# Order of the first loads and of the first group's attention rounds in a one-core kernel: linear attention, then a gated feed-forward

## The chip, the cores and the metric

The kernel runs on one core of one Trainium2 chip. Its engines are PE (matrix products; PEld is the load of its weights), DVE (vector), ACT (activations), POOL, and SP, which here only issues DMAs. DMAs are issued from SP, ACT and POOL. The metric is the device time of one launch in microseconds (us), given as the median of several runs.

## The reference

```python
# q, k, v: 8 x 8 x 576 x 64 (batch, head, row, dim), float32
kv  = einsum('bhsd,bhse->bhde', k, v)          # 64 x 64 per head
out = einsum('bhsd,bhde->bhse', q, kv)
rms = sqrt(mean(out * out, axis=-1) + 1e-06)
x   = out / rms * g_norm                       # then to 4608 x 512
h   = x @ w_in                                 # 512 -> 2048, weights in float64
sp  = maximum(h, 0) + log1p(exp(-abs(h)))
y   = (h * erf(sp)) @ w_out                    # 2048 -> 512
```

## The kernel before, in words

The 4608 rows are worked in groups T. Groups 0 to 7 are the first 512 rows of the eight batches, group 8 gathers the last 64 rows of every batch. Two heads form a pair p, so each group has four pairs. For each group the kernel runs attention, then the two feed-forward products in pieces of 128 of the 2048 columns.

The weights come as float64. For the first group they are turned into float32 piece by piece beside the work: `load_w` fetches a raw piece (L192 for w_in, L197 for w_out), `w_split` takes exponent and mantissa apart (DVE L207, L216; ACT L215, L219), and `w_join` puts them together (DVE L226, L230, L240). Four raw buffers turn, so a load waits for the join four pieces earlier.

Attention of one pair consists of pieces, which the kernel issues one by one:

- `products` (L288): kv of the two heads, 12 products of 64x64 in one PSUM tile `kv_ps` (L297, in the trace 24 passes); for even pairs the transposition of the last 64 rows of two pairs, the tail (L305); DVE copies the two blocks into the block-diagonal `bd_kv` (L312) and the tail into `qT_last` (L315); PE transposes q (L319, four times), ACT copies it out (L320).
- `apply` (L322): the block-diagonal product with the tail (L324) and with q (L325, into `se_ps`); DVE copies the tail's result (L326), ACT squares (L328).
- `mean` (L341): a product with `mean_w` gives the mean of squares (L351); ACT does Ln, Exp and Square (L358, L359, L360).
- `norm` (L364): three DVE operations (L366, L369, L378); the last one writes `xT`.

There is no scheduler: each engine takes its instructions in the order in which the code issues them (`manual_schedule`). For group 0 that order is made by a loop over rounds i (L568):

```python
for i in range(NP + 3):
    for piece, p in ((0, i), (1, i - 1), (4, i - 3), (3, i - 2)):
```

So in round i come `products` of pair i, `apply` of pair i-1, `norm` of pair i-3 and `mean` of pair i-2 (piece 2 isn't used in group 0). After them come the weight steps of `w_rounds` (L559): the first split in round 1, the first join in round 2. The PSUM tiles of q's transposes and of the means share two banks in turn (`banks_0`); `se_ps` has a bank for each pair.

The first loads are issued as follows. `load_pair` (L120) issues q of a pair from SP (L127), and k and v (L136) from ACT for pairs 0 to 2 and from SP after that. `load_last` (L145) issues two heads' tails from SP (L147). POOL first fetches g_norm (L154), then makes the identity `ident` for the transposes, zeroes `bd_kv` (L180) and computes `gm_col` (L182). SP's order is q of pair 0, two tails, q of pairs 1 and 2, two raw pieces of w_in, two more tails, then q, k and v of pair 3. The built program gives the loads of SP and ACT eight completion semaphores in turn, so a load waits until the one eight before it has landed.

A load of q holds 256 KB, of k or v 288 KB, of a tail 32 KB, of a raw piece of w_in 512 KB (the first four) or 1024 KB.

Of the kernel before, what the change touches and what calls it, by code (L numbers as in the profile page):

```python
# [39 lines left out]
FP32 = mybir.dt.float32  # L40
# [20 lines left out]
def kernel(  # L61
# [10 lines left out]
    nc = tc.nc  # L72
    P = 128
    B, H, S, D = q.shape
    DM, DF = moe_w_in.shape[0], moe_w_in.shape[1] // 2
    J = 4
    G = J * P
    R = S - G
    NP = H // 2
# [5 lines left out]
    const = ctx.enter_context(tc.tile_pool(name="const", bufs=1))  # L85
# [12 lines left out]
    ps_o = ctx.enter_context(tc.tile_pool(name="ps_o", bufs=1, space=PSUM))  # L98
# [12 lines left out]
    q_sb, k_sb, v_sb = {}, {}, {}  # L111
# [4 lines left out]
    def chunks(T):  # L116

        return 6 if T == 0 else 5

    def load_pair(i):  # L120
        T, p = divmod(i, NP)
        if T >= B:
            return
        pool = early if i in (2, 3) else kvp
        side = nc.scalar if i < 3 else nc.sync
        t = q_sb[T, p] = pool.tile([P, J, 2, D], FP32, name="q_sb", tag="q")
        nc.sync.dma_start(  # L127
            out=t, in_=q[T, 2 * p : 2 * p + 2, 0:G, :].rearrange("h (p j) d -> p j h d", j=J)
        )
        for name, got, src in (("k", k_sb, k), ("v", v_sb, v)):  # L130
            C = chunks(T)
            rows, rest = divmod(S, C)
            assert rest < 2
            t = got[T, p] = pool.tile([rows + rest, 2, C, D], FP32, name=f"{name}_sb", tag=name)
            heads = src[T, 2 * p : 2 * p + 2]
            side.dma_start(  # L136
                out=t[:rows].rearrange("r h c d -> r h (c d)"),
                in_=heads[:, : S - rest].rearrange("h (r c) d -> r h (c d)", c=C),
            )
            if rest:  # L140
                side.dma_start(
                    out=t[rows:, :, 0], in_=heads[:, S - rest :].rearrange("h r d -> r h d")
                )

    def load_last(T, p):  # L145
        if T < B:
            nc.sync.dma_start(  # L147
                out=q_last[p % 2 * R : p % 2 * R + R, p // 2],
                in_=q[T, 2 * p : 2 * p + 2, G:S, :].rearrange("h r d -> r h d"),
            )  # L150

    g_col = const.tile([P, 1], FP32, name="g_col")
    for i in range(2):
        nc.gpsimd.dma_start(  # L154
            out=g_col[i * D : i * D + D, :], in_=g_norm.rearrange("(d one) -> d one", one=1)
        )
    for i in range(NP - 1):
        load_pair(i)
        if i == 0:
            load_last(0, 0)  # L160
            load_last(0, 1)

    w_in_sb = first_w.tile([P, KC, DF], FP32, name="w_in_sb")
    w_out_sb = first_w.tile([P, FC, DM], FP32, name="w_out_sb")
# [1 line left out]

    ident = const.tile([P, P], FP32, name="ident")
    make_identity(nc, ident)
    mean_w = const.tile([P, P], FP32R, name="mean_w")
    mean_f = early.tile([P, P], FP32, name="mean_f", bufs=1)  # L170
    nc.vector.memset(mean_f, 0.0)
# [4 lines left out]
    nc.vector.memset(exp_col, -896.0 * (1 << 23))  # L176
    eps_col = const.tile([P, 1], FP32, name="eps_col")
    nc.vector.memset(eps_col, EPS)
    bd_kv = const.tile([P, 2, P], FP32, name="bd_kv")
    nc.gpsimd.memset(bd_kv, 0.0)  # L180
    gm_col = const.tile([P, 1], FP32, name="gm_col")
    nc.gpsimd.tensor_scalar(out=gm_col, in0=g_col, scalar1=-0.5, scalar2=None, op0=ALU.mult)  # L182
    x_last = const.tile([P, KC, G], FP32, name="x_last")
# [66 lines left out]
    def w_next(what):  # L250
        i = w_at[what]
        if i < len(w_order):
            w_at[what] = i + 1
            {"load": load_w, "split": w_split, "join": w_join}[what](*w_order[i][1:])
# [14 lines left out]
    def attention(T, p, pools=None):  # L269

        st = {}

        halves = FIRST <= T < B
        bd = bd_kv[:, (T * NP + p) % 2, :]

        q_tail, o_tail = slice(P, 2 * P), slice(2 * P, 2 * P + R)

        def bank(name):
            pool, tag = (pools or {}).get(name, (ps_at, "at"))
            return pool.tile([P, G], FP32, name=name, tag=tag)  # L280

        def square_tile(name):

            if T == 0:
                return gate.tile([P, G], FP32, name=name, tag="h")
            return attp.tile([P, G], FP32, name=name, tag="qT")

        def products():  # L288

            kv_ps = st["kv"] = bank("kv_ps")  # L290
            ks, vs, qs = (x.pop((T, p)) for x in (k_sb, v_sb, q_sb))
            C = chunks(T)
            for c in range(C):
                rows = slice(0, S // C + (c < S % C))
                for i in range(2):
                    s = slice(i * D, i * D + D)
                    nc.tensor.matmul(  # L297
                        kv_ps[s, s],
                        lhsT=ks[rows, i, c],
                        rhs=vs[rows, i, c],  # L300
                        start=(c == 0),
                        stop=(c == C - 1),
                    )
            if p % 2 == 0:
                nc.tensor.transpose(kv_ps[:, q_tail], q_last[:, p // 2], ident)  # L305
            if p == NP - 2:
                for i in range(NP):
                    load_last(T + 1, i)
            st["qT"] = square_tile("qT")
            for i in range(2):  # L310
                s = slice(i * D, i * D + D)
                nc.vector.tensor_copy(out=bd[s, s], in_=kv_ps[s, s])  # L312
            if p % 2 == 0:
                tails[T] = attp.tile([P, P], FP32, name="qT_last", tag="t")
                nc.vector.tensor_copy(out=tails[T], in_=kv_ps[:, q_tail])  # L315
            st["tail"] = tails[T][:, p % 2 * R : p % 2 * R + R]
            qt_ps = bank("qt_ps")
            for j in range(J):
                nc.tensor.transpose(qt_ps[:, j * P : j * P + P], qs[:, j], ident)  # L319
            nc.scalar.copy(st["qT"], qt_ps)  # L320

        def apply():  # L322
            qT, o_ps, kv_ps = st["qT"], bank("se_ps"), st.pop("kv")
            nc.tensor.matmul(kv_ps[:, o_tail], lhsT=bd, rhs=st.pop("tail"), start=True, stop=True)  # L324
            nc.tensor.matmul(o_ps, lhsT=bd, rhs=qT, start=True, stop=True)  # L325
            nc.vector.tensor_copy(out=x_last[:, p, T * R : T * R + R], in_=kv_ps[:, o_tail])  # L326
            st["o"] = o_ps
            nc.scalar.activation(qT, o_ps, AF.Square)  # L328
# [62 lines left out]
        def loads():  # L391
            load_pair(T * NP + p + 2)

        if T == 0:
            return products, apply, halve, mean, norm
        if T == B:
            return lambda: None, square, lambda: None, mean, norm, split

        pieces = ((products,), (apply,), (halve, loads)) if halves else ((products, loads), (apply,), ())
        return (*(partial(chain, *group) for group in pieces), mean, norm, split)  # L400

# [112 lines left out]
    o_ps = {}  # L514
# [34 lines left out]
    def unit(name):  # L549
        return gate.tile([P, G], FP32, name=name, tag=name[0])  # L550


    for _ in range(2):
        w_next("load")
    load_last(0, 2)
    load_last(0, 3)
    load_pair(NP - 1)

    w_rounds = {  # L559
        1: ("split",),  # L560
        2: ("join", "load", "split"),
        3: ("join", "load"),
        5: ("split",),
        6: ("split", "join", "load", "join", "load"),
    }
    banks_0 = {"kv_ps": (ps_at, "at"), "qt_ps": (ps_h, "h"), "ms_ps": (ps_h, "h")}
    first = [attention(0, p, banks_0 | {"se_ps": (ps_o, f"o{p}")}) for p in range(NP)]
    for i in range(NP + 3):  # L568
        for piece, p in ((0, i), (1, i - 1), (4, i - 3), (3, i - 2)):
            if 0 <= p < NP:  # L570
                first[p][piece]()
        if i == 1:
            for _ in range(RAW - 2):
                w_next("load")
            load_pair(NP)
            load_pair(NP + 1)
        for what in w_rounds.get(i, ()):
            w_next(what)
# [65 lines left out]
    for n in range(FIRST * FC + 1):  # L644
        T, f = divmod(n, FC)
# [33 lines left out]
        elif T < FIRST:  # L679
# [10 lines left out]
            for i, c in blocks:  # L690
                nc.tensor.matmul(  # L691
                    plain[i],
                    lhsT=w_in_sb[:, c, i % FC * P : i % FC * P + P],
                    rhs=xT[T][:, c, :],
                    start=(c == 0),
                    stop=(c == KC - 1),
                )
        if T < FIRST:
            if n == whole:
                old_h = acc.tile([P, BATCH, G], FP32, name="h", tag="e")  # L700
            h = hs[n] = old_h[:, n - whole] if n >= whole else unit("h_sb")
# [51 lines left out]
    def part(h, half):  # L753
        return h[:, :, half * 2 * P : half * 2 * P + 2 * P]
# [31 lines left out]
    for m in range(first_batch, batches + 1):  # L786
        T, b = divmod(m, NB)
        todo = []
        if T + 1 < NG:
            todo = list(attention(T + 1, b))  # L790
            if b == 0:
                side = late_r if T % 2 == FIRST % 2 else late
# [28 lines left out]
        if m < batches:  # L821

            pool, tag = (acc, "e") if m % 2 else (wide, "b")
            h = pool.tile([P, BATCH, G], FP32, name="h", tag=tag)
# [22 lines left out]
        for j in range(J):  # L847
# [7 lines left out]
            for half in range(2) if j == 1 and m < batches - 1 else (j,) if j < 2 and m == batches - 1 else ():  # L855
                nc.vector.tensor_tensor(  # L856
                    out=part(h, half), in0=part(h, half), in1=part(s, half), op=ALU.mult
# [38 lines left out]
```

## Time and profile before

| | |
|---|---|
| Runs | 946.79, 948.34, 949.3, 949.31 us |
| Median | 948.82 us |
| Profiled execution | 946.79 us, its span 945.0 us |
| PE, DVE, ACT, POOL busy | 926.1, 740.1, 615.5, 2.4 us |
| Granted PE clock, mean | 0.999 |
| DMA in the span | 259.78 MB, mean 275 GB/s |
| PE busy in 0 to 20, 20 to 40, 40 to 60 us | 11.24, 17.96, 20.00 us |

The times of the profile are from the start of the span of 945.0 us; the run around it took 1.8 us more. PE is the busiest engine, 98% of the span, and most of what it lacks is lost at the start. A busy share is an average over the whole span, so stages have to be looked at one by one. A timeline line gives start, duration, engine, code line, operation, what is written and read, the count of merged instructions, and in brackets the idle time before it and what ended it. A line of windows gives for each engine the busy time in a stretch and the number of instructions, then the granted clock, the mean busy share of the 16 DMA engines and the rate in GB/s.

### The profile page before, as it was taken

What the parts mean: (1) busy time and instruction counts of PE and PEld (TensorE: products, weight loads), DVE (VectorE), ACT (ScalarE), POOL (GpSimd) and SP (SyncE); (2) the same over time, 40 slices, a digit from 0 to 9 for tenths busy, and PEclk for the clock granted to TensorE, in tenths of its full rate; (3) what the DMA queues carried; (4) which work ended last, traced back from release to release, by engine and by line L of the source; (5) the groups of instructions that cost most, each with busy time, mean ns of one, the idle gap of its engine ahead of it and who ended that gap; (6) DMA issues with size and microseconds to landing.
All of it is one profiled execution on the core that took longest, in us unless ns stands there. A gap on an engine that the chain in (4) does not pass through costs nothing.

```text
span 945.0 us, 11743 instructions
## 1 busy us (share of the span) xinstructions
PE 926.1 (98%) x4272; PEld 683.1 (72%) x4272; DVE 740.1 (78%) x1054; ACT 615.5 (65%) x825; POOL 2.4 (0%) x10
## 2 busy tenths in 40 slices
PE   6999999999999999999999999999999999999998
PEld 4444445665688888888888888888888888878886
DVE  3979958888577788777788888878887877777667
ACT  4889876777666666666666666666666666665552
POOL 1000000000000000000000000000000000000000
PEclk9999999999999999999999999999999999999999
DMA  9856505899699998998899889988797779768872
GB/s 261 283 166 214 162 7 219 309 343 339 221 339 339 310 332 293 315 313 278 291 295 316 290 295 313 313 302 293 266 339 272 265 250 348 286 246 310 335 271 60
DMA packets 111842, 259.78 MB, mean 275 GB/s; under 512 B 43864, under 2 KB 69544, under 8 KB 111784
## 3 DMA queue, kind: packets, MB, share of 16 engines
q1 hardware_dynamic: 110152, 256.73, 78.5%
q10 hardware_dynamic: 1568, 2.29, 0.8%
q8 instruction: 34, 0.56, 0.2%
q14 instruction: 24, 0.20, 0.1%
q0 software_dynamic: 64, 0.00, 0.0%
HBM read 224.40 MB, written 34.60 MB: 274 GB/s over the span
## 4 chain that ended last, share of the span: by engine, by line
PE 87%; ACT 5%; DVE 5%; DMA 2%; issue 1%; SPq 0%; DVEq 0%
PE n_ps L462 45%; PE m_ps L462 23%; PE o_ps L520 8%; PE h_ps L691 3%; PE se_ps L325 3%; PE kv_ps L297 2%; PE qt_ps L319 1%; DMA w_raw<-in_moe_w_in_dram 1%; ACT w_e L215 1%; ACT w_m L219 1%; DMA v_sb<-in_v_dram 1%; PE ms_ps L346 1%; PE ms_ps L347 1%; ACT L103 1%; ACT s_sb L719 1%
## 5 line engine op out<-in xcount | busy, mean ns | idle before, releaser
L462 PE MATMUL n_ps<-x_forms,w_in_parts 128*128 128x512 f32 x896 | 233.2, 402 | 1.5 <-DVE x_forms L408 0.7
L462 PE MATMUL n_ps<-w_out_parts,g_forms 128*128 128x512 f32 x928 | 231.3, 391 | 0.0
L462 PEld LDWEIGHTS n_ps<-w_out_parts,g_forms 128*128 128x128 f32 x928 | 174.2, 188 | 38.5 <-issue 1.4
L462 PEld LDWEIGHTS n_ps<-x_forms,w_in_parts 128*128 128x128 f32 x896 | 166.7, 188 | 45.3 <-issue 9.1
L838 ACT ACTIVATE s<-h 128x512 f32<-128x512 f32 x112 | 71.0, 633 | 180.2 <-DVE h L445 180.2
L445 DVE TENSOR_TENSOR h<-m_ps,h 128x512 f32<-128x512 f32 x116 | 79.8, 688 | 60.9 <-ACT h L836 41.4
L462 PE MATMUL m_ps<-w_out_parts,g_forms 128*128 128x512 f32 x464 | 124.2, 389 | 0.0
L462 PE MATMUL m_ps<-x_forms,w_in_parts 128*128 128x512 f32 x448 | 120.0, 389 | 0.0
L520 PE MATMUL o_ps<-w_out_sb,h_sb 128*128 128x512 f32 x224 | 100.8, 592 | 0.3 <-DVE h_sb L642 0.3
L462 PEld LDWEIGHTS m_ps<-w_out_parts,g_forms 128*128 128x128 f32 x464 | 87.1, 188 | 18.1
L462 PEld LDWEIGHTS m_ps<-x_forms,w_in_parts 128*128 128x128 f32 x448 | 84.1, 188 | 17.7
L445 DVE TENSOR_TENSOR e<-m_ps,e 128x512 f32<-128x512 f32 x116 | 80.2, 692 | 18.3 <-PE m_ps L462 11.2
L440 DVE SCALAR_TENSOR_TENSOR e<-n_ps,e 128x512 f32<-128x512 f32 x88 | 60.3, 685 | 39.9 <-PE n_ps L462 39.9
L520 PEld LDWEIGHTS o_ps<-w_out_sb,h_sb 128*128 128x128 f32 x224 | 42.3, 190 | 48.9 <-issue 46.6
L411 DVE SCALAR_TENSOR_TENSOR g_forms<-g_forms 128x1024 fp32r<-128x1024 f32 x58 | 71.1, 1225 | 2.0
L408 DVE TENSOR_TENSOR g_forms<-h,g_forms 128x1024 fp32r<-128x1024 f32 x58 | 70.6, 1217 | 1.7 <-ACT g_forms L405 1.4
L836 ACT ACTIVATE h<-n_ps 128x512 f32<-128x512 f32 x112 | 65.5, 585 | 3.9 <-PE n_ps L462 3.9
L405 ACT ACTIVATE g_forms<-h 128x1024 fp32r<-128x1024 f32 x58 | 58.8, 1058 | 12.5 <-PE m_ps L462 9.8
L856 DVE TENSOR_TENSOR h<-h,s 128x1024 f32<-128x1024 f32 x56 | 65.9, 1218 | 0.7 <-ACT s L842 0.7
L691 PE MATMUL h_ps<-xT,w_in_sb 128*128 128x512 f32 x144 | 64.9, 594 | 0.8 <-DVE w_in_sb L240 0.6
L106 ACT ACT_TABLE_LOAD x44 | 56.5, 1283 | 0.8
L842 ACT ACTIVATE s<-s 128x1024 f32<-128x1024 f32 x56 | 56.2, 1052 | 0.3
(98 smaller groups left out, 1012.9 us busy)
## 6 DMA issues: line engine op xcount, KB each, us to landing
w_out_parts<-w_out SPq DMA_DIRECT2D x116, 768.0 KB
w_in_parts<-w_in SPq DMA_DIRECT2D x112, 768.0 KB
w_in<-w_new SPq DMA_DIRECT2D x16, 768.0 KB
q_sb<-in_q_dram SPq DMA_DIRECT2D x32, 256.0 KB
w_raw<-in_moe_w_out_dram SPq DMA_DIRECT2D x8, 1024.0 KB
out_dram<-e SPq DMA_DIRECT2D x32, 256.0 KB
k_sb<-in_k_dram SPq DMA_DIRECT2D x28, 287.5 KB
v_sb<-in_v_dram SPq DMA_DIRECT2D x28, 287.5 KB
```

Source lines behind the costliest of these rows:

```text
L106: nc.scalar.preload_act_table_set("softplus")
L405: nc.scalar.activation(high, x, AF.Copy, scale=1.0 + 2.0**-13)
L408: nc.vector.tensor_tensor(out=low, in0=x, in1=high.bitcast(FP32), op=ALU.subtract)
L411: nc.vector.scalar_tensor_tensor(out=both, in0=low.bitcast(FP32), scalar=SHIFT, in1=high.bitcast(FP32), op0=ALU.mult, op1=ALU.add,)
L440: nc.vector.scalar_tensor_tensor(out=out_, in0=ps, scalar=scale, in1=out_, op0=ALU.mult, op1=ALU.add)
L445: nc.vector.tensor_tensor(out=out_, in0=ps, in1=out_, op=ALU.add)
L462: nc.tensor.matmul(ps, lhsT=weights(form, k), rhs=moving(form, k), start=(form == forms[0] and k == 0), stop=(form == forms[-1] and k == 3),)
L520: nc.tensor.matmul(o_ps[j], lhsT=g[:, j * P : j * P + P], rhs=w_out_sb[:, f, :], start=(f == 0), stop=last,)
L691: nc.tensor.matmul(plain[i], lhsT=w_in_sb[:, c, i % FC * P : i % FC * P + P], rhs=xT[T][:, c, :], start=(c == 0), stop=(c == KC - 1),)
L836: nc.scalar.activation(h[:, i], n_ps, AF.Copy, scale=SHIFT - 1.0)
L838: nc.scalar.activation(s[:, i], h[:, i], AF.Softplus)
L856: nc.vector.tensor_tensor(out=part(h, half), in0=part(h, half), in1=part(s, half), op=ALU.mult)
```

## The change

It touches the first loads, the first group's rounds, and nothing after them: behind the first group's attention each engine's instructions stand in the same order as before.

1. `load_pair` is cut into `load_part`, which issues q, k or v alone, from a queue that is named. The first three pairs' loads are issued in the order k, v, q. SP gets k and q of pair 0, q of pair 1, and k, v and q of pair 2. ACT gets v of pair 0, k of pair 1, the first two tails, and v of pair 1. The order behind that on SP is two raw pieces of w_in and then q, k and v of pair 3, as before.
2. POOL makes `ident` and zeroes `bd_kv` first, then fetches the other two tails and g_norm.
3. In group 0 q's transposes come ahead of the tail's, and the product with q ahead of that with the tail.
4. The rounds' order becomes `norm` of pair i-3, `mean` of pair i-2, `apply` of pair i-1, `products` of pair i. The first split, join and load come one round later.
5. Eight 128x128 products of `mean_w` with `mean_f` into a tile `idle` that nobody reads stand ahead of all others on PE.

```diff
+    def load_part(i, name, side=nc.sync):
...
+    for i, name, side in (
+        (0, "k", nc.sync),
+        (0, "v", nc.scalar),
+        (0, "q", nc.sync),
+        (1, "k", nc.scalar),
+        (1, "v", nc.scalar),
+        (1, "q", nc.sync),
+        (2, "k", nc.sync),
+        (2, "v", nc.sync),
+        (2, "q", nc.sync),
+    ):
+        load_part(i, name, side)
+        if (i, name) == (1, "k"):
+            for j in range(2):
+                load_last(0, j, side)
...
+    ident = const.tile([P, P], FP32, name="ident")
+    make_identity(nc, ident)
+    bd_kv = const.tile([P, 2, P], FP32, name="bd_kv")
+    nc.gpsimd.memset(bd_kv, 0.0)
+    for i in range(2, NP):
+        load_last(0, i, nc.gpsimd)
     g_col = const.tile([P, 1], FP32, name="g_col")
...
-    for i in range(NP - 1):
-        load_pair(i)
-        if i == 0:
-            load_last(0, 0)
-            load_last(0, 1)
...
+            def transpose_q():
+                qt_ps = bank("qt_ps")
+                for j in range(J):
+                    nc.tensor.transpose(qt_ps[:, j * P : j * P + P], qs[:, j], ident)
+                return qt_ps
+            qt_ps = transpose_q() if T == 0 else None
             if p % 2 == 0:
                 nc.tensor.transpose(kv_ps[:, q_tail], q_last[:, p // 2], ident)
...
-            nc.tensor.matmul(kv_ps[:, o_tail], lhsT=bd, rhs=st.pop("tail"), start=True, stop=True)
-            nc.tensor.matmul(o_ps, lhsT=bd, rhs=qT, start=True, stop=True)
+            both = [(kv_ps[:, o_tail], st.pop("tail")), (o_ps, qT)]
+            for ps, x in reversed(both) if T == 0 else both:
+                nc.tensor.matmul(ps, lhsT=bd, rhs=x, start=True, stop=True)
...
-    load_last(0, 2)
-    load_last(0, 3)
     load_pair(NP - 1)
     w_rounds = {
-        1: ("split",),
-        2: ("join", "load", "split"),
-        3: ("join", "load"),
+        2: ("split",),
+        3: ("join", "load", "split"),
+        4: ("join", "load"),
         5: ("split",),
         6: ("split", "join", "load", "join", "load"),
     }
+    idle = ps_o.tile([P, P], FP32, name="idle", tag="o3")
+    def keep_warm(n):
+        for _ in range(n):
+            nc.tensor.matmul(idle, lhsT=mean_w.bitcast(FP32), rhs=mean_f, start=True, stop=True)
+    keep_warm(8)
     for i in range(NP + 3):
-        for piece, p in ((0, i), (1, i - 1), (4, i - 3), (3, i - 2)):
+        for piece, p in ((4, i - 3), (3, i - 2), (1, i - 1), (0, i)):
             if 0 <= p < NP:
                 first[p][piece]()
```

More of the change, by code (lines that the diff above doesn't have):

```diff
@@ L118, in chunks @@
         return 6 if T == 0 else 5
-    def load_pair(i):
+    def load_part(i, name, side=nc.sync):
         T, p = divmod(i, NP)
-        if T >= B:
-            return
         pool = early if i in (2, 3) else kvp
[L125 to L130, printed above, removed]
+        if name == "q":
+            t = q_sb[T, p] = pool.tile([P, J, 2, D], FP32, name="q_sb", tag="q")
+            side.dma_start(
+                out=t, in_=q[T, 2 * p : 2 * p + 2, 0:G, :].rearrange("h (p j) d -> p j h d", j=J)
+            )
+        else:
+            got, src = (k_sb, k) if name == "k" else (v_sb, v)
             C = chunks(T)
@@ L143, in load_pair, with load_last @@
                 )
-    def load_last(T, p):
+    def load_pair(i):
+        if i < B * NP:
+            for name in "qkv":
+                load_part(i, name)
+    def load_last(T, p, side=nc.sync):
         if T < B:
-            nc.sync.dma_start(
+            side.dma_start(
                 out=q_last[p % 2 * R : p % 2 * R + R, p // 2],
@@ L150, in load_last @@
             )
+    for i, name, side in (
[13 more added lines that the diff above has]
+                load_last(0, j, side)
+    w_in_sb = first_w.tile([P, KC, DF], FP32, name="w_in_sb")
+    w_out_sb = first_w.tile([P, FC, DM], FP32, name="w_out_sb")
+    ident = const.tile([P, P], FP32, name="ident")
[4 more added lines that the diff above has]
+        load_last(0, i, nc.gpsimd)
     g_col = const.tile([P, 1], FP32, name="g_col")
@@ L156 @@
         )
-    for i in range(NP - 1):
-        load_pair(i)
-        if i == 0:
-            load_last(0, 0)
-            load_last(0, 1)
[L163 to L168, printed above, removed]
     mean_w = const.tile([P, P], FP32R, name="mean_w")
@@ L178 @@
     nc.vector.memset(eps_col, EPS)
-    bd_kv = const.tile([P, 2, P], FP32, name="bd_kv")
-    nc.gpsimd.memset(bd_kv, 0.0)
     gm_col = const.tile([P, 1], FP32, name="gm_col")
@@ L316, in products @@
             st["tail"] = tails[T][:, p % 2 * R : p % 2 * R + R]
-            qt_ps = bank("qt_ps")
-            for j in range(J):
-                nc.tensor.transpose(qt_ps[:, j * P : j * P + P], qs[:, j], ident)
+            if T > 0:
+                qt_ps = transpose_q()
             nc.scalar.copy(st["qT"], qt_ps)
```

## The prediction

> **What bounds the kernel now.** I read the windows of busy time first, to see which stage can pay for an edit that touches only the first group's attention and the loads before it.
>
> ```profile
> 15.00:20.00 5.00, 4.42 (x55) 2.80 (x56) 2.90 (x8) 3.60 (x7) 0.00 (x0) 1.00 1.13 303
> 20.00:30.00 10.00, 8.66 (x37) 4.10 (x33) 9.42 (x19) 9.76 (x17) 0.00 (x0) 1.00 0.61 186
> ...
> 60.00:87.00 27.00, 25.18 (x100) 11.33 (x99) 25.73 (x33) 22.98 (x30) 0.00 (x0) 1.00 0.57 176
> 87.00:300.00 213.00, 212.70 (x825) 128.81 (x826) 165.33 (x249) 152.70 (x219) 0.00 (x0) 1.00 0.70 246
> ```
>
> The columns are PE, PEld, DVE, ACT and POOL busy, the granted clock, the DMA share, GB/s. From 87 us on PE is full (212.70 of 213) and stays so. From about 17 to 87 us DVE and ACT are full in turn. So the edit can only move the moment at which this saturated train starts; whatever it moves is carried to the end unchanged, since the instructions after it and their count stay the same. The waits of DVE between 16.9 and 37.3 us confirm the train: 2.4 us in all, of which 2.0 is the wait that ends at its start.
>
> ```profile
> DVE bd_kv L312 <- PE kv_ps L305: 2.0, 1, 2.0
> DVE x_last L326 <- PE kv_ps L324: 0.2, 1, 0.2
> DVE qT_last L315 <- PE kv_ps L324: 0.2, 1, 0.2
> ```
>
> The timeline shows what starts it, pair by pair:
>
> ```profile
> 5.84 1.55 PE L297 MATMUL kv_ps<-v_sb,k_sb 96*64 96x64 f32 x24 [5.84 <-DMA v_sb<-in_v_dram]
> ...
> 11.03 1.55 PE L297 MATMUL kv_ps<-v_sb,k_sb 96*64 96x64 f32 x24 [1.54 <-DMA v_sb<-in_v_dram]
> ...
> 15.23 0.92 PE L297 MATMUL kv_ps<-v_sb,k_sb 96*64 96x64 f32 x24
> ...
> 16.89 0.46 DVE L312 COPY bd_kv<-kv_ps 64x64 f32<-64x64 f32 x2 [2.02 <-PE kv_ps L305]
> ...
> 19.43 0.92 PE L297 MATMUL kv_ps<-v_sb,k_sb 96*64 96x64 f32 x24 [0.18 <-DMA v_sb<-in_v_dram]
> ...
> 20.45 0.45 DVE L312 COPY bd_kv<-kv_ps 64x64 f32<-64x64 f32 x2
> ```
>
> Two gates are to be seen. Gate 1 is pair 2's block copy at 16.89: from there DVE runs dense to the last of the first four weight joins, which ends at 37.22 (16.9 to 37.22 = 20.3 us; at 37.86 ACT takes over, having waited 2.43 us for DVE). Gate 2 is pair 3's copy at 20.45, which follows v of pair 3. The chain of waits names that load:
>
> ```profile
> 4.35 9.24 DMA w_raw<-in_moe_w_in_dram
> 13.61 5.68 DMA v_sb<-in_v_dram
> ```
>
> v of pair 3 lands at 13.61 + 5.68 = 19.29. And there is one hole in the stream of loads:
>
> ```profile
> 4.00:4.75 0.75, 0.00 (x0) 0.00 (x0) 0.00 (x0) 0.00 (x0) 0.00 (x0) 1.00 1.03 280
> 4.75:6.00 1.25, 0.16 (x3) 0.19 (x5) 0.00 (x0) 0.00 (x0) 0.00 (x0) 1.00 0.43 123
> 6.00:7.00 1.00, 1.00 (x22) 1.00 (x23) 0.00 (x0) 0.00 (x0) 0.00 (x0) 1.00 1.05 310
> ```
>
> **What the Trainium skill says.** "DMA: Bandwidth & Descriptors", section "Issuing engines are not separate DMA queues": loads issued from SP, ACT and POOL run on the same 16 DMA engines, and several issuers save only the time of issuing. The trace agrees: the DMA share is 1.05 or more in each slice I took from 6 to 20 us, so apart from the hole the loads are bound by bytes, not by queues. "TensorE: Matmul & The Clock Gate", Part 1: the array runs at half its clock until it has been busy for about one window of 3.4 us. The trace agrees: the same 24 passes of L297 take 1.55 us at 5.84 and 11.03, and 0.92 at 15.23 and 19.43; the switch comes only after PE was busy from 11.03 on without a gap.
>
> **The change part by part.**
>
> *Order of the first loads.* k and v of pair 0 now lead two queues. They hold 0.58 MB; before, that much had been moved by 4.0 us (the rates of 2-3 and 3-4 us are 239 and 328 GB/s). ACT's queue shows the last packets of v at about 5.1 and PE starts at 5.84, so 0.7 to 0.9 from last packet to start: pair 0 now starts at about 4.9, 0.9 earlier. q of pair 0, k of pair 1 and two tails (0.61 MB) follow at 280 GB/s: 4.0 + 2.2 + 0.7 = 6.9. v of pair 1 waits for k of pair 0 (the build gives SP's and ACT's loads eight completion semaphores in turn; each load waits for the load eight before it), and comes after 2.02 MB in all: 4.0 + 1.44/0.28 + 0.7 = 9.8, against 11.03. For pair 3 nothing is removed: its v stands behind the same 4.5 MB (four pairs, tails, two weight pieces) in both. Only the hole can be saved: 1.25 us at 123 instead of 280 GB/s is 0.7 us. So v of pair 3 lands at 19.29 - 0.7 = 18.6; bounds 18.0 (pairs 0 and 1 also mix better) and 19.3 (a hole comes elsewhere, since SP now issues v of pair 2 only when q of pair 0 has landed).
>
> *Tails and g_norm on POOL.* POOL's two DMAs take 1.23 us to issue now and g_norm's column is used at 7.05. With the identity and the zeroed blocks ahead, and four DMAs, gm_col comes some 3 us later, about 10; it is needed at the first xT, about 17. The identity is ready earlier (it was at 3.0). Nothing, hidden.
>
> *Eight products without use.* Between 1.65 us (mean_w ready) and k and v at 4.9, PE was idle. A 128x512 mean product is 2 passes of 0.43; of 128 columns at half clock I estimate 2 x 0.21, eight of them 3.4 us, ending at 5.0: at most 0.2 us of delay. With pair 0's products right behind them PE is busy from 1.65 to 6.5, one window's worth, so the full clock should come by about 8 and not at 14.7.
>
> *Order of the rounds.* PE now does mean, then block-diagonal product of pair p, before kv of pair p+1. Pair 0: q at 6.9, transposes 0.6 to 1.06, tail 0.3, block copy 0.46, product 0.9 to 1.6, tail product 0.2: about 10.0. v of pair 1 is there at 9.8. From kv of pair 1 at full clock: kv 0.92 + transposes 0.60 + mean 0.90 + product 0.91 + 0.17 + kv 0.92 + transposes 0.60 + tail 0.30 = 5.3, so gate 1 opens at about 15.4, not 16.89. Pair 2's loads end 2.6 MB into the stream, 4.0 + 2.0/0.28 + 0.7 = 11.8; they and the POOL tails are there by then. Then the copy of qT (0.58), mean (0.90), product (1.08): PE is free for pair 3 at 17.7, before v lands at 18.6. Gate 2 follows 1.02 after kv's start, as before (19.43 to 20.45): 18.7 + 1.0 = 19.7.
>
> *What DVE has left.* From the starts of one row to the next: split 0.67, join 1.93, norm 2.11, block copy 0.46, qT_last 0.24, x_last 0.14. After gate 1 before: 19.75 dense plus 0.6 of gaps. After the change one split (0.67) has moved behind gate 1 and one x_last (0.14) ahead of it: 20.3 + 0.6 = 20.9. Behind gate 2 stand block copy, 4 joins, 3 norms, 3 splits, x_last = 16.66 + 0.4 = 17.1 (before 16.8, since norm of pair 0 now comes ahead of it, and a join and a split behind). Gate 1 gives 15.4 + 20.9 = 36.3, gate 2 gives 19.7 + 17.1 = 36.8. The later one counts: 37.2 - 36.8 = 0.4 to 0.5 us saved. ACT does not come last there: its Ln, Exp, Square of pair 1 end at about 20.2 (used at 22.7), split of piece 1 at 23.9 (used at 25.0), those of pair 2 at 25.8 (used at 26.9).
>
> *New waits.* Mean of pair 1 takes the bank of pair 2's q transposes and so waits for their copy on ACT (the 0.58 above); behind it stand pair 2's product and pair 3's kv, which wait for v longer. Transposes of pair 3 wait for the first DVE row of norm 0, at about 17, needed at 19.5. The weight loads of later pieces are issued at 30.77 and after, from SP's own order; the first that DVE waits for has 1.6 us of slack (DVE's w_e at 38.70 is used by ACT at 41.00). Nothing.
>
> **Sum.** The profiled execution took 946.79 (span 945.0, 1.8 around it) and would take 946.3. The median of the four runs is 948.82 and its runs reach from 946.79 to 949.31; the profiled one is the fastest. On the median the change gives 948.3.
>
> **The rivals.**
> - The order of loads brings nothing to pair 3 (0.2). For it: DMA share above 1 nearly throughout. Gate 2 stays at 20.45 and DVE's 17.1 end at 37.5: 0.3 slower, 949.1.
> - Both gates early (0.2). Pair 1 starts at 9.5, gate 1 at 14.9, v of pair 3 by 17.7: end at 35.8, saved 1.4, with the PE clock and a later mix of loads up to 2.2; 947.2. For it: k packets beside q packets flow faster than alone (310 at 6-7 us, 264 at 10-11). Against it: gate 2 would have to gain 1.6.
> - Slower: PE keeps half its clock (0.18). The new order makes PE a chain in which each pair waits for the last one's product. If the eight products do not fill a window and the switch comes at 14.7 as now, kv, transposes and mean of pair 1 take 1.55 + 1.06 + 1.57 from 10.4, and gate 1 comes at 17.5: 17.5 + 20.9 = 38.4, 1.2 slower; at half clock until pair 2, gate 1 at 18.3 and 1.9 slower. I take 1.4: 950.2. It decides from a gate 1 later than 37.2 - 20.9 = 16.3.
>
> **How the numbers follow.** My case has 0.42. A measurement of this kernel tells about 0.2%, 1.9 us, from no change. No case lies beyond it in its middle; the second rival does so with its far end (0.08) and the third with its own (0.06). The median of a few runs moves by some 0.8 us, which adds 0.12 on the side of faster and 0.09 on the other. Faster 0.2, same 0.65, slower 0.15. The range takes in the second and third rivals' middles: 946.7 to 950.2.
>
> **What would show it.** Right: first L297-type products at about 4.9, pair 1's at about 10 in 0.92 to 1.2 us, block copy of pair 2 at 15 to 16, v of pair 3 at 18 to 19, the fourth join's end at 36.4 to 37.0, and the first wholly full PE window about 0.5 earlier. Wrong: 24-pass groups of 1.55 us after 9 us (the clock), DVE waiting for pair 3 beyond 20.2, or a time that moves by more than the first 38 us moved.

## The result, and the profile after

The changed kernel takes 949.09 us (median of 41 runs, 947.62 to 949.53), the kernel before 947.66 beside it (61 runs). The ratio is 1.0011, 95% interval 1.0006 to 1.0015: slower by 1.0 us by the ratio and 1.4 us by the medians. Its profiled execution took 947.75 us (span 945.9) against 946.79 before (span 945.0). It is one of the quicker ones: 29 of the 41 took 948.89 us or more, all but two of these at a mean granted clock of 0.993 to 0.996 against its 0.998, so most executions had PE at half clock for longer than the trace below shows.

PE, DVE and ACT up to the end of the train in the timeline of the changed kernel (lines left out are marked; start, duration, engine, line, work, and in brackets the idle time ahead of it and what ended it; kv is now L314, q's transposes L324, the tail L330, the block copy L337, the products L350, the mean L376):

```profile
1.68 3.79 PE L595 MATMUL idle<-mean_f,mean_w 128*128 128x128 f32 x16 [1.68 <-DVE eps_col L197]
5.63 1.36 PE L314 MATMUL kv_ps<-v_sb,k_sb 96*64 96x64 f32 x24 [0.17 <-DMA v_sb<-in_v_dram]
7.94 0.63 PE L324 MATMUL qt_ps<-ident,q_sb 128*128 128x128 f32 x4 [0.95 <-DMA q_sb<-in_q_dram]
8.88 0.30 PE L330 MATMUL kv_ps<-ident,q_last 128*128 128x128 f32 x1 [0.32 <-DMA q_last<-in_q_dram]
9.92 1.92 PE L350 MATMUL se_ps<-qT,bd_kv 128*128 128x512 f32 x2 [0.74 <-DVE bd_kv L337]
...
12.09 1.53 PE L314 MATMUL kv_ps<-v_sb,k_sb 96*64 96x64 f32 x24
...
17.76 0.47 DVE L337 COPY bd_kv<-kv_ps 64x64 f32<-64x64 f32 x2 [1.32 <-PE kv_ps L330]
...
20.37 0.92 PE L314 MATMUL kv_ps<-v_sb,k_sb 96*64 96x64 f32 x24
...
21.47 0.45 DVE L337 COPY bd_kv<-kv_ps 64x64 f32<-64x64 f32 x2
...
28.01 1.13 PE L376 MATMUL ms_ps<-qT,mean_w 128*128 128x512 f32 x2 [2.79 <-ACT qT L353]
...
37.65 0.69 DVE L257 TENSOR_TENSOR w_in_sb<-w_e,w_m 128x512 f32<-128x512 f32 x1
...
38.98 1.15 ACT L232 ACTIVATE w_e<-w_e,exp_col 128x1024 int32<-128x1024 int32 x1 [2.43 <-DVE w_e L224]
```

The end of the train before:

```profile
36.53 0.69 DVE L240 TENSOR_TENSOR w_in_sb<-w_e,w_m 128x512 f32<-128x512 f32 x1
...
37.86 1.15 ACT L215 ACTIVATE w_e<-w_e,exp_col 128x1024 int32<-128x1024 int32 x1 [2.43 <-DVE w_e L207]
```

Gate 1, pair 2's block copy, is at 17.76 and not at 16.89. From there DVE is dense: no other wait until the fourth join, which starts at 37.65 (before 36.53) and ends at 38.3. ACT has waited the same 2.43 us when it takes over, at 38.98 (before 37.86). So of the 1.12 us by which the fourth join is late, 0.87 are lost at gate 1 and carried on, and 0.25 come behind it, where the train now holds one split more. Gate 2 at 21.47 has no wait and decides nothing. Pair 0's product takes 1.92 us and pair 1's kv 1.53: PE runs at half its clock there. The windows of busy time show the clock (PE, PEld, DVE, ACT and POOL busy, granted clock, DMA share, GB/s):

```profile
3.24:6.65 3.41, 3.24 (x30) 2.97 (x31) 0.00 (x0) 0.00 (x0) 0.69 (x2) 1.00 1.16 271
6.65:10.06 3.41, 1.41 (x16) 0.93 (x14) 0.70 (x3) 0.58 (x1) 0.22 (x1) 1.00 1.17 280
10.06:13.47 3.41, 3.41 (x28) 2.25 (x28) 0.26 (x2) 0.60 (x1) 0.00 (x0) 0.50 1.15 305
```

The clock record begins with the switch to full at 6.65, so the 1.00 of the first line is no record; the 0.50 of the third is one. The eight products and pair 0's kv nearly filled a window of 3.41 us (3.24), and the full clock followed. In the next one PE waited for q, for the tail and for the block copy (the brackets above), worked for 1.41 us, and the clock fell back, just when the chain of products began.

### The profile page after: what moved, and what is told of

Read it like the earlier page. It is cut to its first block, busy times and chain, and to the rows that moved or that the text cites. A ratio compares the mean times of both kernels' runs of the same rounds, so it can differ in the third digit from the quotient of the medians.

```text
span 945.9 us, 11779 instructions
## 1 busy us (share of the span) xinstructions
PE 929.1 (98%) x4288; PEld 686.4 (73%) x4288; DVE 740.2 (78%) x1054; ACT 615.8 (65%) x825; POOL 3.5 (0%) x12
## 4 chain that ended last, share of the span: by engine, by line
PE 88%; DVE 5%; ACT 5%; DMA 1%; issue 1%; ACTq 0%; DVEq 0%
PE n_ps L487 45%; PE m_ps L487 23%; PE o_ps L545 8%; PE h_ps L722 3%; PE se_ps L350 3%; PE kv_ps L314 2%; PE qt_ps L324 2%; ACT w_e L232 1%; DMA q_last<-in_q_dram 1%; ACT w_m L236 1%; ACT L103 1%; PE ms_ps L372 1%; PE ms_ps L371 1%; PE ms_ps L376 1%; ACT s_sb L750 1%
```

## The experiments

Theory A: the clock that fell back costs the time. B: the new order of rounds costs it, since each pair's kv now stands behind the last pair's product. C: the late loads do, v of pair 3 above all. D and E, on why pair 3 can be late, and F, that the later weight steps cost the time, came later. Each kernel was timed beside the one before; the ratios are to that.

### Keeping the clock: e1_bridge

```diff
+            if (T, p) == (0, 0):
+                keep_warm(4)
             qt_ps = transpose_q() if T == 0 else None
+            if (T, p) == (0, 0):
+                keep_warm(1)
             if p % 2 == 0:
                 nc.tensor.transpose(kv_ps[:, q_tail], q_last[:, p // 2], ident)
+            if (T, p) == (0, 0):
+                keep_warm(3)
```

> The changed kernel with eight more unused products in pair 0: four after kv, one after q's transposes, three after the tail's, so that PE has no gap between 1.7 and 10 us and should keep its full clock. Theory A (PE falls back to half clock at 10.06 because it idled before, and that makes the first group's chain late): the block-diagonal product of pair 0 takes about 1.0 instead of 1.92 us, kv of pair 1 starts at about 11.1 and takes 0.92 instead of 1.53, gate 1 (pair 2's block copy) comes at 16.1 to 16.5 instead of 17.76, the fourth join ends at 36.7 to 37.1 instead of 38.3; 1.0 to 1.5 us less than the changed kernel. Theory B (the order of the rounds is late by itself, its copies between PE's products being exposed): gate 1 stays at 17.2 or later and the time within 0.5 us of the changed kernel. Theory C (q and tails of pair 0 land too late): gate 1 moves by less than 0.6 us, since the products start no earlier.

Measured: 947.23 us, ratio 0.9993 (0.9984 to 1.0001), 1.9 us below the changed kernel. Its windows and its timeline:

```profile
6.55:9.97 3.42, 3.22 (x33) 2.73 (x30) 0.54 (x3) 0.59 (x1) 0.22 (x1) 1.00 1.18 278
9.97:13.38 3.41, 3.39 (x34) 2.15 (x35) 0.87 (x4) 1.18 (x2) 0.00 (x0) 1.00 1.14 294
```

```profile
9.99 1.10 PE L356 MATMUL se_ps<-qT,bd_kv 128*128 128x512 f32 x2
...
11.18 0.92 PE L314 MATMUL kv_ps<-v_sb,k_sb 96*64 96x64 f32 x24
...
16.24 0.47 DVE L343 COPY bd_kv<-kv_ps 64x64 f32<-64x64 f32 x2 [1.32 <-PE kv_ps L334]
...
20.53 0.92 PE L314 MATMUL kv_ps<-v_sb,k_sb 96*64 96x64 f32 x24 [1.61 <-DMA v_sb<-in_v_dram]
...
21.49 0.46 DVE L343 COPY bd_kv<-kv_ps 64x64 f32<-64x64 f32 x2 [1.45 <-PE kv_ps L314]
```

With the gaps filled PE is busy for 3.22 us of the window from 6.55 to 9.97, the clock stays, the product falls from 1.92 to 1.10 us and gate 1 comes at 16.24. A holds for the clock, for gate 1 and for the median. Its fourth join was forecast to end at 36.7 to 37.1 and did not: in this profiled execution (948.62) v of pair 3 came late, gate 2 has a wait of 1.45, and the fourth join starts at 38.24, later than the changed kernel's 37.65.

### The order, the products and the loads: e2, e3, e4, e6

e2_old_rounds is the changed kernel with

```diff
-        for piece, p in ((4, i - 3), (3, i - 2), (1, i - 1), (0, i)):
+        for piece, p in ((0, i), (1, i - 1), (4, i - 3), (3, i - 2)):
```

and the weight steps of before; e3_no_warm is the changed kernel with `keep_warm(0)`; e4_rounds_only is the kernel before with the new order and weight steps alone; e6_old_no_warm is e2 and e3 together, so that only the loads are left.

> The changed kernel with the rounds' order and the weight steps of the kernel before; loads, POOL's order, the eight products and q's transposes first stay. Theory B: gate 1 comes at 15.5 to 16.5, the joins end at 37.0 or earlier, the time is 0.2 to 1 us below the kernel before. Theory A: PE still falls to half clock in pair 0, but products of pair 1 no longer stand behind pair 0's block-diagonal product, so gate 1 is at 16.3 to 17.3 and the time near the kernel before, within 0.4 us. Theory C: as late as the changed kernel, 1 us above the kernel before.

> The changed kernel without the eight unused products. Theory A: the full clock that they bought (6.65 to 10.06 us) fell on a stretch in which PE mostly waited; without them PE is at half clock until 13 to 15 us; gate 1 at 17.5 to 18.3, the time within 0.4 us of the changed kernel. Theory B and C: the same time within 0.2 us.

> The kernel before with the new order of the rounds and the later weight steps alone; loads as before, no unused products. Theory B: gate 1 at 18 us or later, since pair 0's tails land at 8.1 and v of pair 1 at 11.0; 1 us or more above the kernel before. Theory A: half clock until 14.7 in a serial chain, gate 1 at 17.7 to 18.5, also above the kernel before by 0.8 to 1.5. Theory C (the loads are what is late): no slower than the kernel before, within 0.3 us.

> Only the loads' new order is left of the change: rounds of before, no unused products. Theory A with B (with the old order gate 1 doesn't stand behind pair 0's product, so half a clock costs little): PE at half clock until 13 to 15 us, gate 1 at 16.8 to 17.3, gate 2 at 20.4 to 20.9, time as e2 within 0.3 us, 947.1 to 947.6. If the products are what e2 gained by: 0.5 to 1 us above e2. If the loads bring nothing: as before.

Measured: e2 947.13 (0.9992, 0.9983 to 1.0002), e3 949.15 (1.0012, 1.0005 to 1.0018), e4 949.52 (1.0014, 1.0006 to 1.0021), e6 947.36 (0.9996, 0.9988 to 1.0004). Pair 1's kv and gate 1 in e2, at half clock from 8.85 to 15.67:

```profile
9.91 1.55 PE L314 MATMUL kv_ps<-v_sb,k_sb 96*64 96x64 f32 x24 [0.56 <-DMA v_sb<-in_v_dram]
...
16.86 0.46 DVE L337 COPY bd_kv<-kv_ps 64x64 f32<-64x64 f32 x2 [1.39 <-PE kv_ps L330]
```

The same in e3, whose first switch to full comes at 14.02:

```profile
10.61 2.04 PE L350 MATMUL se_ps<-qT,bd_kv 128*128 128x512 f32 x2 [0.74 <-DVE bd_kv L337]
...
12.90 1.41 PE L314 MATMUL kv_ps<-v_sb,k_sb 96*64 96x64 f32 x24
...
18.45 0.47 DVE L337 COPY bd_kv<-kv_ps 64x64 f32<-64x64 f32 x2 [1.32 <-PE kv_ps L330]
```

e3 is as slow as the changed kernel: the eight products bring nothing that the median shows (between the two profiled executions gate 1 differs by 0.7 us, 18.45 against 17.76). e2 and e6 lie at the kernel before or up to 0.8 us below it: the loads do no harm that shows, which speaks against C as the cause of the slowdown, and their gain is too small to be told apart. With the old order pair 1's kv starts as soon as v is there (9.91) and fills the time in which pair 0's block copy is waited for; in the changed kernel it starts at 12.09 and in e3 at 12.90. So new order and weight steps together cost 2.0 us in the changed kernel (949.09 to 947.13) and about 1.6 alone (e4). e1, with the new order at full clock, is as fast as e2, with the old one at half: what the new order costs, the clock gives back.

### Full clock with the old order, and pair 3 earlier: e5, e7, e8

e5_old_bridge is e2 with the bridge of e1. e7_bridge_v3early and e8_old_bridge_v3early are e1 and e5 with

```diff
-    for _ in range(2):
-        w_next("load")
+    w_next("load")
     load_pair(NP - 1)
+    w_next("load")
```

> The changed kernel's loads with the rounds of before, and with the eight unused products of e1 (4, 1 and 3 of them in the gaps behind pair 0's kv, q transposes and tail), so that PE stays at full clock from about 6.6 us on. Theory A with C (with the old order the clock moves gate 1, but v of pair 3 then decides): kv of pair 1 takes 0.92 at about 10, gate 1 (block copy of pair 2) comes at 14.2 to 15 instead of the 16.86 of e2, gate 2 stays at 20.4 to 20.9, PE waits for v of pair 3; the fourth join ends as in e2, time equal to e2 within 0.3 us, 947.1. Theory A alone (the clock decides in any order): time falls by 1.5 us or more against e2, 945.6. Theory B (the order of rounds costs time by itself): this kernel is faster than e1 at the same clock.

> e1 with pair 3's q, k and v loaded ahead of the second weight piece and not behind it. Theory C (with full clock v of pair 3 decides): PE no longer waits for v of pair 3, gate 2 comes at 20 or earlier with no wait, DVE is dense from gate 1 at 16.2, the fourth join ends at 16.2 + 20.5 = 36.7 instead of 38.9 in e1's profiled run (38.3 in the changed kernel's), time 946.9 or less. If v of pair 3 isn't what holds e1: time as e1, 947.2, and the second piece, which comes 3 us later, may hold the second split (then 947.5 or more).

> e5 with pair 3's q, k and v ahead of the second weight piece. If gate 1 and gate 2 are both early (C): gate 1 at 14.2 to 15, gate 2 at 17 to 18.5, the fourth join ends at 35 to 36 instead of 37.2 before, time 945.5 to 946.5: the fastest of all. If the second weight piece then decides (it lands at about 20): DVE waits at the second split and the gain is under 0.5 us against before, 947.3. Theory B: faster than e7 at the same clock and with the same loads.

Measured: e5 950.77 (1.0027, 1.0016 to 1.0038; six executions), e7 946.51 (0.9990, 0.9981 to 0.9998), e8 948.57 (1.0006, 0.9998 to 1.0015). e5 left no trace that can be read. e7 came as C said: gate 1 at 16.35, gate 2 at 20.06 without a wait, fourth join at 36.25, faster than before; against e1 the intervals overlap. e5 and e8 are misses: with the old order the full clock did harm. In e8's timeline v of pair 3 comes at 19.14 though it is loaded earlier than in e1, and kv and transposes run at half clock:

```profile
19.14 1.28 PE L314 MATMUL kv_ps<-v_sb,k_sb 96*64 96x64 f32 x24 [2.37 <-DMA v_sb<-in_v_dram]
20.35 1.12 PE L324 MATMUL qt_ps<-ident,q_sb 128*128 128x128 f32 x4
...
23.32 0.22 DVE L357 COPY x_last<-kv_ps 128x64 f32<-128x64 f32 x1 [2.15 <-PE kv_ps L356]
```

Two things meet here. PE got through its early work so fast that it stood idle before pair 3 and lost the clock (theory E). And the trace has a transfer that no line of the kernel issues: one packet of 16 KB on a queue of instructions, in e8 at 14.74, inside the loads (theory D). I take it for PE's instructions, since in all sixteen traces it comes when PE has begun 102 to 131 products, at times from 14.74 to 22.27.

### Fewer instructions for the same PE time: e9 to e12

e9_wide is e1 with the unused products up to 384 columns wide: 14 passes in place of 32. e10_wide_old is the same for e5, e11_wide_old_v3early for e8, and e12_wide_old_v3early_w is e11 with the changed kernel's later weight steps.

```diff
     def keep_warm(n):
-        for _ in range(n):
-            nc.tensor.matmul(idle, lhsT=mean_w.bitcast(FP32), rhs=mean_f, start=True, stop=True)
+        while n > 0:
+            w = min(n, 3) * P
+            nc.tensor.matmul(
+                idle[:, :w], lhsT=mean_w.bitcast(FP32), rhs=warm_f[:, :w], start=True, stop=True
+            )
+            n -= 3
```

> e1 with the same PE time in unused products, but in up to 384 columns instead of 128, so 14 passes instead of 32. Theory D (each pass of an unused product brings PE's next 16 KB fetch of instructions forward, which came at 17.07 us in e1, at 19.41 in the changed kernel with 16 passes and at 21.50 before with none; when it falls into the load of v of pair 3 it holds up one DMA engine by 1.0 to 1.2 us): the fetch comes at 18.5 to 19.5, behind the last packets of v of pair 3, which end at about 18.0 instead of 19.4; gate 2 at 20.0 to 20.5; gate 1 at 16.2 as in e1; time 0.3 to 1 us below e1, 946.3 to 946.9. If the fetch has nothing to do with it: v of pair 3 and time as in e1, 947.2.

> e5 (rounds of before at full clock) with the wide unused products of e9. Theory D: e5's 950.3 comes from the fetch inside the loads; with 14 passes instead of 32 it comes later than v of pair 3, and the time falls to that of e2 or below, 946.3 to 947.2. Theory E (the old order at full clock is slower for another reason: PE stands idle before pair 3, loses its clock there, and pair 3 runs at half): the time stays at 948.5 to 950.5, and the trace shows half clock from about 20 us.

> e8 with the wide unused products. Theory D: the fetch leaves 14.7 us for 17 or later, v of pair 3 lands at about 17.3 instead of 19.1, PE's idle time before pair 3 falls from 2.4 to 0.5 to 1 us and the clock stays; what is left is DVE's wait for the second weight piece (1.8 us, at 20.0), time 947 to 947.8. Theory E: PE still idles over 1.5 us before pair 3 and falls to half clock; time 948.5.

> e11 with the changed kernel's later weight steps (first split in round 2), so that the second weight piece isn't waited for at 18 us. If that wait was what held e8: gate 1 at 15 to 15.5, gate 2 at 18.5 to 19.3, no DVE wait over 0.5 us behind gate 2, fourth join's end at 36 to 36.8, time 946.0 to 946.7, the fastest of all or equal to e7. If pair 3 comes at half clock or late: 947.5 or more.

Measured: e9 947.19 (0.9992, 0.9984 to 1.0000), e10 948.79 (1.0011, 1.0002 to 1.0021), e11 946.10 (0.9984, 0.9977 to 0.9990), e12 948.38 (1.0007, 0.9998 to 1.0015). e11 differs from e8 only in the form of these products (the first starts 0.26 us later, behind the zeroing of their operand) and is 2.5 us lower in the median (2.1 by the ratios). Its median is the lowest of all kernels here, 1.7 us below before; e7 is next, and their intervals overlap. e9 is no faster than e1 in the median, so with the new order D is not borne out, though in its profiled execution (946.54) gate 2 had no wait. e10's profiled execution (950.17) shows E. Its timeline and windows:

```profile
20.16 1.55 PE L316 MATMUL kv_ps<-v_sb,k_sb 96*64 96x64 f32 x24 [3.60 <-DMA v_sb<-in_v_dram]
21.63 1.12 PE L326 MATMUL qt_ps<-ident,q_sb 128*128 128x128 f32 x4
```

```profile
15.70:19.10 3.40, 0.86 (x2) 0.03 (x1) 2.97 (x7) 3.34 (x7) 0.00 (x0) 1.00 1.09 315
19.10:22.50 3.40, 2.34 (x28) 2.26 (x29) 0.45 (x2) 0.84 (x2) 0.00 (x0) 0.51 0.93 281
```

A window with 0.86 us of work before pair 3, and the next at half clock. The packet fell at 16.72 in e10, again inside v of pair 3. E seems not to strike in each execution: five of e10's 13 took 947.1 to 947.7, and with fewer passes the median is 2.0 us below e5's, so with the old order the form of the unused products counts too. e12 missed by 2 us: gate 2 came at 18.97 as forecast and the time still rose; the first join and a split now stand behind gate 2 and DVE idles ahead of it (its waits between 10 and 21 us are 7.1 us, in e11's profile 5.9).

### Order and weight steps apart: g13, g14, g15

g13_weights_early is the changed kernel with only the weight steps of before, g15_old_weights_late with only the order of before; g14_wide_weights_early is e9 with the weight steps of before.

```diff
-        2: ("split",),
-        3: ("join", "load", "split"),
-        4: ("join", "load"),
+        1: ("split",),
+        2: ("join", "load", "split"),
+        3: ("join", "load"),
```

> The changed kernel with the weight steps of before (first split in round 1, first join in round 2), its round order kept. With e2 (both undone, 947.13) and the changed kernel (949.09) it divides the 2.0 us between the two edits. Theory B (the order costs it, since pair 1's kv stands behind pair 0's product at half clock; the steps only move one split of 0.67 us from idle time of DVE to behind gate 1): gate 1 stays at 17.5 to 18, the fourth join starts 0.6 to 0.7 earlier, at 37.0, time 948.4. Theory F (the later weight steps cost it, since DVE then stands idle before gate 1 with nothing to do): time 947.1 to 947.5.

> e9 (new order at full clock) with the weight steps of before. Theory B: one split moves into DVE's idle time before gate 1 at 16.6, the first join comes before norm of pair 0; the fourth join starts 0.6 us earlier than e9's 36.47, time 945.9 in a profiled run and 946.5 in the median. Theory F: 945.2 or less. If ACT, which does half of the split and waits for the first weight piece until 14.2 to 14.8, then delays the copy of pair 2's q and the means: time as e9 or above, 947.2.

> The changed kernel with the round order of before and its own later weight steps. Theory B: as e2 but for one split, 947.1 to 947.8. Theory F: DVE idles before gate 2 (about 20.8) with the first join and second split still to come behind it, fourth join 1.5 to 2 us later than e2's 36.89, time 948.4 to 949.1.

Measured: g13 950.36 (1.0025, 1.0015 to 1.0034), g14 947.87 (0.9999, 0.9991 to 1.0007), g15 949.79 (1.0022, 1.0013 to 1.0032). Neither B nor F alone explains the 2.0 us: either edit alone is clearly slower than neither (e2, 0.9992), and in the medians 0.7 to 1.3 us slower than both together (1.0011), though there the intervals touch or overlap. g15 went F's way, and further: its fourth join came 3.0 us behind e2's. So each order does best with its own weight steps. g14 gained nothing on e9; its full clock came only at 11.21 and its gate 1 at 17.98, so it says little of the steps. In g13's timeline gate 1 is earlier than in the changed kernel (17.31), but join and split stand ahead of pair 3's block copy, which comes at 22.95, and DVE waits later. PE is at half clock there from 23.67 to 33.91, and what of the waits is the late copy and what the clock was not separated:

```profile
22.95 0.45 DVE L337 COPY bd_kv<-kv_ps 64x64 f32<-64x64 f32 x2
...
33.37 0.69 DVE L391 SCALAR_TENSOR_TENSOR qT<-ms_ps,qT 128x512 f32<-128x512 f32 x1 [1.67 <-ACT qT L385]
```

### One number for all of them

The start of the fourth join and the time of the same profiled execution:

| kernel | gate 1 | gate 2 | fourth join | time | difference |
|---|---|---|---|---|---|
| before | 16.89 | 20.45 | 36.53 | 946.79 | 910.26 |
| changed | 17.76 | 21.47 | 37.65 | 947.75 | 910.10 |
| e1 | 16.24 | 21.49 | 38.24 | 948.62 | 910.38 |
| e2 | 16.86 | 20.83 | 36.89 | 946.98 | 910.09 |
| e3 | 18.45 | 22.16 | 38.36 | 948.49 | 910.13 |
| e4 | 19.18 | 23.36 | 39.65 | 949.99 | 910.34 |
| e6 | 16.37 | 20.34 | 37.23 | 947.31 | 910.08 |
| e7 | 16.35 | 20.06 | 36.25 | 946.31 | 910.06 |
| e8 | 15.33 | 20.72 | 38.67 | 948.76 | 910.09 |
| e9 | 16.58 | 20.29 | 36.47 | 946.54 | 910.07 |
| e10 | 14.91 | 21.74 | 40.13 | 950.17 | 910.04 |
| e11 | 15.46 | 21.21 | 37.01 | 947.11 | 910.10 |
| e12 | 14.96 | 18.97 | 38.50 | 948.64 | 910.14 |
| g13 | 17.31 | 22.95 | 39.41 | 949.41 | 910.00 |
| g14 | 17.98 | 23.63 | 39.14 | 949.27 | 910.13 |
| g15 | 16.91 | 20.29 | 39.86 | 949.97 | 910.11 |

The time is the start of the fourth join plus 910.0 to 910.4 us, whatever was changed. Neither gate gives it alone (e12 has two early gates): what counts is how long DVE stood idle before that join, at the gates and elsewhere. Each row is one execution: e11's median is 1 us below the time shown, the changed kernel's 1.3 us above it.

## Why the prediction was wrong

Right was the frame: DVE's train up to the fourth join sets the time, it moves as a whole, and from gate 1 on it was dense (20.6 us to the join's end, 20.9 predicted). The table shows it for sixteen kernels.

The step that failed: "With pair 0's products right behind them PE is busy from 1.65 to 6.5, one window's worth, so the full clock should come by about 8 and not at 14.7", and with it "From kv of pair 1 at full clock ... = 5.3, so gate 1 opens at about 15.4". The switch came, at 6.65. But I took the full clock as lasting once reached, with no term for losing it again. It fell back at 10.06, and product, tail product and kv of pair 1 ran at half. Of gate 1's 2.4 us (15.4 to 17.76) e1 takes away 1.5 (to 16.24), by the clock alone: 0.9 up to the start of pair 1's kv (12.09 to 11.18), 0.6 after it. The sum of the chain itself was good at full clock: 5.06 us in e1 (11.18 to 16.24) against 5.3.

A second term was mis-sized. I let pair 0 be done at "about 10.0"; at full clock it was at 11.2 (kv of pair 1 in e1). q was used at 7.94 and not at 6.9, the tail at 8.88; k and v of pair 0 were used at 5.63 and not at 4.9. It was not the bytes that were late: the last packets of k and v started at 4.14 and 4.17, close to my 4.0. The step from the last packet to PE's start, which I took as 0.7 to 0.9 from the kernel before (5.03 to 5.84 there), took 1.5 here; why was not tried. The two errors meet: by my sum PE would have waited 0.9 us in the window after the switch (0.4 for q, 0.46 for the block copy), and it waited 2.0 (0.95 for q, 0.32 for the tail, 0.74 for the block copy). Whether the clock would have stayed with q on time was not tried.

Gate 2 was mistaken in its cause. The last packets of v of pair 3 started at 18.07, close to what a landing at 18.6 asked for, but PE reached it only at 20.37, behind pairs 1 and 2. A later PE had taken the place of the load.

The rival "PE keeps half its clock" came close in its numbers: gate 1 at 17.76 against its 17.5, the fourth join 1.1 us later against its 1.2. I had given it 0.18 because the eight products seemed to fill a window. They did, so its condition did not hold; the half clock came on the same stretch by another way, and that the numbers agree is in part luck. So is it that 949.09 lies between the 946.7 and 950.2 of the prediction: that range was drawn around a median of 948.82 from four runs, and 61 runs put the kernel before at 947.66.

The Trainium skill ("TensorE: Matmul & The Clock Gate", section "Why this matters for your kernels") asks for no idle gaps over about 3 us to keep the clock. In this trace the length of a gap does not tell: no gap in the window that lost the clock was longer than 0.95 us, while a gap of 2.79 us ahead of the mean at 28.01 lost nothing. What the lost window had was a low busy share, 1.41 of 3.41.

The later weight steps I counted as one split of 0.67 us moved behind gate 1. For the change as it stands that was about right: 0.25 us of the 1.12 came behind gate 1. g13, which moves the steps back, is no faster. For e11 the same steps cost 2.3 us (e12).

Not settled: where PE was at half clock in the executions that make the changed kernel's median, since the one trace is of a quicker one; how much of e1's and e9's spread (946.3 to 948.6 in both) is the instruction packet; and what the new loads alone are worth: e6's interval reaches from 1.1 us of gain to 0.4 of loss.

## What to carry to other kernels

Work that only warms PE is worth its place when it fills the gaps behind it as well: count PE's busy share window by window up to the point where the clock matters. Before putting a chain of dependent products ahead of independent work, price it at half clock too; the independent work was what hid the waits. When two edits go together (an order and the steps placed by it), undo each alone as well as both: here each alone had a higher median than both.

## What the runs showed of the hardware that was not expected

- PE's clock is switched on a grid of 3.41 us. Between one switch and the next lay 3.41, 6.83, 10.24, 13.65 or 20.48 us in the first 45 us of the sixteen traces, all multiples of 3.41. The grid does not start with PE's work: with the eight products starting at 1.68 or 1.94, the first switch to full came at any time from 5.43 to 7.22 in ten traces. What goes with a switch is PE's busy time in the window of the grid before it. Over the sixteen traces the full clock was always lost after a window with at most 1.41 us of PE work and always kept with 1.78 or more; between 1.50 and 1.77 both occurred. From half it always rose after 3.24 us or more and never after less than 3.05.
- The gap of 2.79 us ahead of 28.01 in the changed kernel lost nothing because the grid cuts it: the window from 23.71 to 27.13 still held 1.51 us of work.
- Without the transposes (q's and the tail's) the windows that lost the full clock have at most 1.33 us of work and those that kept it at least 1.51, with no overlap; the lost window of the changed kernel then has 0.49. But from half the clock rose after 2.57 us counted so (before, 11.29 to 14.71) and did not after 3.18 (g14, 4.38 to 7.80). So the traces leave it open whether transposes count.
- So the same eight products did not always bring the full clock. In g15's execution, where they straddled two windows, with 2.72 us of work from 0.99 to 4.40 and 2.61 from 4.40 to 7.81, it came only at 14.64, and in g14's at 11.21. A window view shows 1.00 before the first record of the clock, so that half clock is to be read from the durations there (1.55 for the 24 passes).
- With unused products the 16 KB packet of instructions comes earlier. It holds a DMA engine for 1.0 to 1.3 us. It came at 21.50 to 22.27 in the four kernels without such products, at 19.41 in the changed kernel with 16 more passes and at 17.07 in e1 with 32. Where it fell into v of pair 3 (e1, e10) the last packets of that load started at 19.41 and 19.05, elsewhere with the same loads at 17.0 to 18.7 (the changed kernel, e2, e3, e6, g13, g14, g15 and e9; in e9 it came at 17.84, at the very end of the load). With pair 3 loaded earlier it is alike: 18.01 in e8, where the packet came at 14.74, and 16.8 to 17.3 in e7, e11 and e12, where it came at 17.05 or later, at the end of the load or behind it. This is what the traces show side by side; the packet was not moved by itself.
